# A three-stage attention and feed-forward kernel: a new order for TensorE, a new planner table, ones as letters of the order

## The chip, the cores and the metric

The kernel runs on one core of one Trainium2 chip. The metric is the device time of one execution in microseconds (us). Five engines work side by side, each through its own queue and in that queue's order: PE (TensorE, matmuls), DVE (VectorE), ACT (ScalarE), POOL (GpSimd) and SP (SyncE, which here only starts transfers).

## The reference

```python
q_pool = q.reshape(B, H, S // 2, 2, D).mean(axis=3)      # B=2, H=8, S=1152, D=64
scores = np.matmul(q_pool, k.transpose(0, 1, 3, 2)) / np.sqrt(D)
attn = np.exp(scores - scores.max(-1, keepdims=True))
attn = attn / (attn.sum(-1, keepdims=True) + 1e-09)
x = np.matmul(attn, v)                                   # 16 heads of 576 x 64
x = x.transpose(0, 2, 1, 3).reshape(1152, 512)
h = x @ moe_w_in                                         # 512 -> 2048
g = (a0 + a1*h + a2*h**2 + a3*h**3) / (1 + abs(b0)*abs(h) + abs(b1)*h**2 + 1e-06)
x = g @ moe_w_out                                        # 2048 -> 512
xn = x / sqrt(mean(x**2) + 1e-06) * rms_g
g = xn @ w_gate; val = xn @ w_val                        # 512 -> 1536 each
out = (g * sigmoid(g) * val) @ moe2_w_out                # 1536 -> 512
```

## The kernel before, in words

The program has an attention stage (to about 259 us in the profile), a first feed-forward stage, a normalisation and a second feed-forward stage. The feed-forward matmuls multiply pairs of numbers split into a high and a low half, three products each (`three`, L599).

Attention works on 16 heads in 8 pairs. A pair has 9 tiles of 128 query rows against 1152 keys, so there are 72 tiles, and two tiles are in flight at a time, each with its own three PSUM banks (`hid`, here `s_ps`). One tile goes: PE multiplies queries by keys (letters A and C of the order, L919); DVE takes the negated row maximum (`nm`, L951, 1152 columns); ACT takes the exponential with the row sum (`p`, L957); PE transposes the result in 64-column blocks (letters T and 2, L973); DVE and ACT copy the transposed blocks to `pt` (L1009 and L1006). When a head's 576 rows stand in `pt`, PE multiplies them by the values: nine steps a head, letter V (L1078, into the PSUM tile `av`). Before a head begins, its keys and its pooled queries are transposed on PE: letter P (L832; half of it goes to the bank `prep`, half to a corner of the second score tile's third bank), and each half is copied to `kT` or `qT` by DVE or ACT (`copy_ways`, L697 and L700). The pooled queries `qp` are one addition per head (L759). At a pair's end a row of reciprocals is transposed (L1111, L1125) to divide the output.

In the gaps DVE, ACT and POOL convert the weights of the later stages (`weight_ops`, `spill_ops`; tiles `wc`, `wraw`, `win_*`, `wout_*`, `spill`); none of this starts before the operation `later`, which is the exponential of tile 4.

The order of the work is planned when the program is built. Each piece of work is an `Op` with an engine (or several `ways`), an estimated cost, a due time and its dependences. `SHIFTS` moves the due time of each Op, `WAYS` fixes the way of some, and `order` emits the Ops one by one. PE's order in attention is not left to the planner: the string `PE_ORDER` gives it, one letter per Op, and each Op depends on the one before it. Where the string has `PTT2` (two tiles' transposes with no V ahead of them, at five places after the first tile), `attention` puts matmuls of a tile of ones by itself with no use for the result (`f_ones`, L1219): three ahead of the first T and two ahead of the second.

Two tiles are called a round below: round n holds tiles 2n and 2n+1, counted from 0.

Of the kernel before, what the change touches and what calls it, by code (L numbers as in the profile page):

```python
# [8 lines left out]
F32 = mybir.dt.float32  # L9
# [10 lines left out]
def attention_moe_moe2_kernel(  # L20
# [18 lines left out]
    nc = tc.nc  # L39
# [235 lines left out]
    def weight(w, u):  # L275
# [13 lines left out]
        "6QPGR_NgNPP@DORIESuPF?W6YP/LhPP]bRPOPkYN@Sc6ENPUPOePD8XJSTAU]dXyPidQdTwRbTt_PI>;SWlR8bSRPpPX[u(mSH(R"  # L289
        "d9X4PPUs3MyEPPRPPIyPONtQE]PyMKNPY]yFPPAX]UHPs^PKIZOVItBPHSQfJPn?Y*MZPKeK:PChPkBTKTLGXWPPPNV;]SGWbGPY"  # L290
        "TGIVOMSPPPPSPA?FM]FNP]CXPPhPPvPJLHST@PJPdPCsPp8PUZPHAWKVLL=KKSRUSJ?NRGPT_PPKwPUMERVHyyPMPVG]HD6PvDTP"
        "PYJE4UNg;KcN;GP<VD)P?PAKQSELPP]PRPYPZZPWQLUPKhPPYNAZPN>QOI(IQMPAYPPRBYDS@H[OVPGLPSQNSRS@SbfPQFLTMNGI"
        "QHa6PX[KNPPUUDMFS_PUWCPOUCPVPPPPbdJPJNPPPR:bW]FP@POrXMZ7PPXU[P4PDUXP_PRP@TbPWaPJQIOMGAVKHPAZPHM5VTJp"
        "?RTNRP3OVcPTN[gFLhJS[P6E(i`IPPIMPPCP@KL@S]_W1P_YNRoQPPPcFKDSjEH6HMdLXP>JEWUYU]OPP=cKKPnU]RL65@xXGWLR"
        "HPP1PPdK_On_RPWlITPQPKP[bMiPQWUQPb`N^WK;ZSQPQ<eOCMO>MIQPP]PVPPL_UR?:RIPXPKcV]PGPIPHSSPPPD[hPmPRPTPN;"
        "PRGPWQPUPkgUHBPcHGZJaZPXZRMZQQSPTNWPXHWJP(DP>?PQ)P=`NMY(PObNUTIbPNyRPNPQd]WK<PLPRPTE3GPYKOXSK?PPNPP;"
        "ZT@BCPSPi_TNNWPFb^ISJMISPPDPO[PLQPP8UYPPcPMnPITPPJLJKPTPPONPWPPRS:RPPDSPHJNPRSPNX4Z^PcP7DLOSPIHPPdPK"
        "MJeI`IPdPLKUPTWbTPEPRQlH]CZXHsaPPPPhK[PMUYQJhPGR)UePVT_RSKNS[PAeMEWPPPZQOPPcPXLSMaQ.QB]WTV_PPPSP?PKp"
        "^NPOCPPjNPIEFJWSSOGMQSPE`?PGPIPGUNQQM^HP](oYPPPjXXTP,J`APBMHEONHPWZONMQ>@ZX6PbPRPy[IOPNPPPPQmPSPQL^L"
        "XMOZLSLKFDYPIPmPPIHcrhZTXPD2MPWVP:UVPiYSCVO[SPUPSKP]PTITd<H[cOUODLGJPHPkCN6<XPCLPPLMPVPP6P]ZPPURGVTP"  # L300
        "KZY@bVPWPHPRVyZuPPPVK[APDkIPPUPPPIyYTuRDPVVI;MZjS_XM7[SHH?VyFL^IEP`VPSOR7PNPPPPPPE]MC7@ZVRZHQZPcPVB?"
        "Z>PWUIvPSR_JPPWcNaFV@]PO^HIYePPO@NPfRLTPQrWUPPUPmPY^GRKNPWcPTPYPJX;TP>PORPERQP<P]NZPPPPPPPPPPPNPyEKP"
        "PMPDDMYW_TP@[HPM[I<SMVKb`PP^PEZRAPPrLOXNP_@*?PQRPX^KYSBHPNPPQPJ=JTPQPPXPuJWvWPIGSPHPPIEODLID1PUWT^LQ"
        "PRPWPgPHNGLKFlP<KSC9FVCPLSDWP-KPPS]jQNyY6LE@PONTAU;JYP`UVQcPQKITPPPQAxPQdDP8y*AP6QOSFNPPPRTNDGJUeMHP"
        "PQ`DXKDFIKOKVI5BRR<hVB_PPYNNTPLhPPOK@GEPONTN^QSECEQPH1PRP@VPKP;ZXKPPHFTHSPPPYgKM(RXlPBNP[PLbmK:>NePX"
        "JQbPOPB:P`SUoPZ59UUVPUPX<KFkPYYQDZ[PGDyPyRBH<hf`M;LuK?LZLVPkUBTPQON>GOG3hPPYLPPOPRPP[[XhaPjZPCSTHPfN"
        "TX+Id8XPdPPPPGWTLbP0EPP8^MGEMOIPPPPO7(D7BDYPU_@YPJPUP^`PRHJPTPUUPOS]VPGPPPM8eLP<YPRNPP`SPPMFJQ;JKPKN"
        "MPPNPP`]KPPXXPPNPNOCQTPP(yVZJPPVBQP?JO(Q:aXPNPPPPIPaPFOM=XPUKRQCLL<QG:MDXXPPZPNobmfEO[P?WVQOPRPP]YPN"
        "DSP`PQGPPQE[SAP=PPMNvtPJT@PJQ=y`ddjPS?EFP_PVWPPOPPcLPJTMUJMGS^ZIG>mP.KWQSfQHMKRWQZPHUETWZRfSPJ>PPPPu"
        "NPFSNKPKnP7USRPQP:P_EV;[lDISSRLPPePFTTMPSPP1^=R[R]WXWJUjEMPJCVVPNZWAPKPVPTPcpJTBOdbGPPD]HRXPRPpQP[MS"  # L310
        "IPEQ6PPZKNKdGSOPrXSPPPXaPP[PPPGP[[HPa8PudKWU`PSPPQ_LSVPPP`DLPg]PPF=jPU_ULacKdPMPP^:jP)hJUXPWX=P^FTWH"
        "PMPUXLXLXUPFNUdPPPPsPPFNINPPQPP9LQ8RPHMPdPPPLJWDLTUHL]OMQQPSMPLSPDMPfVUXPPXYQPDyT]PPQPdRyZbPAWPPKBT;"
        "PC=PTTXL9PNPcQASWPYUHJEmYQdgOPP@BSN]PPMXP^/UP[PJPP9PeP^WNiPUUXYNMUPSE;(YPOL@HEL6SO_RCPOPiPS<nPNQMPW_"
        ";[PTPLMIP1OCyb-CP]PSC^P@i_PKFJMaGKON_OLPPQ?TkWO7NPPPPTqPPoLCFR]SNParDPJOPEWP,PNIP]NLQ@E7ePV]IOV;kNP]"
        "TPTPLPJPZ`MJTPPPHZAPKPPTTC"
# [1381 lines left out]
```

## Time and profile before

| | |
|---|---|
| median of 3 runs | 693.15 us (692.87 to 693.76) |
| the profiled execution | 692.14 us |
| its span, first to last instruction | 690.3 us |
| PE busy | 672.7 us, 97% of the span, 5457 instructions |
| DVE busy | 536.0 us, 78% |
| ACT busy | 406.7 us, 59% |
| POOL busy | 229.2 us, 33% |
| PE's granted clock, mean of the core | 0.998 of full speed |

Times are microseconds from the first instruction. A matmul's end is modelled in this profile, and matmuls overlap, so a stretch in which PE is "busy" need not be one in which it does as much as it could. An entry like `[1.61 <-ACT p L957]` says that the engine stood idle for 1.61 us before this instruction, and that the last thing it waited for was ACT's instruction of line 957 that writes `p`.

### The profile page before, as it was taken

What the parts mean: (1) busy time and instruction counts of PE and PEld (TensorE: products, weight loads), DVE (VectorE), ACT (ScalarE), POOL (GpSimd) and SP (SyncE); (2) the same over time, 40 slices, a digit from 0 to 9 for tenths busy, and PEclk for the clock granted to TensorE, in tenths of its full rate; (3) what the DMA queues carried; (4) which work ended last, traced back from release to release, by engine and by line L of the source; (5) the groups of instructions that cost most, each with busy time, mean ns of one, the idle gap of its engine ahead of it and who ended that gap; (6) DMA issues with size and microseconds to landing.
All of it is one profiled execution on the core that took longest, in us unless ns stands there. A gap on an engine that the chain in (4) does not pass through costs nothing.

```text
span 690.3 us, 13519 instructions
## 1 busy us (share of the span) xinstructions
PE 672.7 (97%) x5457; PEld 595.2 (86%) x5457; DVE 536.0 (78%) x706; ACT 406.7 (59%) x665; POOL 229.2 (33%) x226
## 2 busy tenths in 40 slices
PE   7899999999999999999999999999999999999998
PEld 6677777767767678999999999999999999989996
DVE  4789899898987978999897889667677257845744
ACT  3787888898889778997555666155233233311210
POOL 2125316756664652421111353055142011312200
PEclk9999999999999999999999999999999999999999
DMA  7433536676653525224115003201335012421103
GB/s 214 145 117 120 146 98 210 198 223 205 192 193 141 196 111 196 78 77 151 41 33 172 31 24 129 62 1 33 115 99 153 30 32 91 129 85 59 34 0 138
DMA packets 54062, 77.69 MB, mean 113 GB/s; under 512 B 6512, under 2 KB 36464, under 8 KB 54000
## 3 DMA queue, kind: packets, MB, share of 16 engines
q1 hardware_dynamic: 53712, 76.50, 34.3%
q8 instruction: 43, 0.70, 0.4%
q10 hardware_dynamic: 288, 0.33, 0.1%
q14 instruction: 19, 0.16, 0.1%
HBM read 62.40 MB, written 14.42 MB: 111 GB/s over the span
## 4 chain that ended last, share of the span: by engine, by line
PE 88%; DVE 6%; ACT 4%; issue 1%; DMA 1%; POOL 0%; SPq 0%; DVEq 0%; ACTq 0%; POOLq 0%
PE hid L599 35%; PE accp L599 25%; PE hid L919 10%; PE av L1078 9%; PE hid L973 7%; DVE nm L951 3%; ACT p L957 2%; DVE pt L1009 1%; PE hid L832 1%; PE prep L1125 1%; DMA qn<-in_q_dram 1%; PE prep L832 1%; DVE acc L1486 0%; DVE qp L759 0%; ACT m_p L1289 0%
## 5 line engine op out<-in xcount | busy, mean ns | idle before, releaser
L599 PE MATMUL hid<-x_hi,win_hi 128*128 128x384 f32 x480 | 161.6, 337 | 1.7 <-issue 0.9
L599 PE MATMUL hid<-x_hi,win_lo 128*128 128x384 f32 x480 | 160.6, 335 | 0.0
L599 PE MATMUL hid<-x_lo,win_hi 128*128 128x384 f32 x480 | 154.8, 335 | 0.0
L951 DVE TENSOR_REDUCE nm<-hid 128x1 f32<-128x1152 f32 x72 | 96.6, 1356 | 13.4 <-PE hid L919 10.2
L957 ACT ACTIVATE p<-hid,nm 128x1152 f32<-128x1152 f32 x72 | 87.9, 1221 | 29.3 <-DVE nm L951 26.6
L599 PEld LDWEIGHTS hid<-x_hi,win_hi 128*128 128x128 f32 x480 | 90.1, 188 | 3.6 <-issue 1.2
L919 PE MATMUL hid<-kT,qT 64*128 64x256 f32 (+3 forms) x800 | 91.3, 372 | 1.2 <-ACT qT L697 1.1
L599 PEld LDWEIGHTS hid<-x_lo,win_hi 128*128 128x128 f32 x480 | 89.6, 188 | 0.9
L599 PEld LDWEIGHTS hid<-x_hi,win_lo 128*128 128x128 f32 x480 | 90.1, 188 | 0.0
L973 PEld LDWEIGHTS hid<-ident,p 64*128 64x128 f32 x1296 | 52.6, 140 | 36.0 <-ACT p L957 21.9
L919 PEld LDWEIGHTS hid<-kT,qT 64*128 64x128 f32 (+1 forms) x800 | 73.7, 179 | 10.0 <-ACT qT L697 1.6
L1078 PE MATMUL av<-pt,vn 128*64 128x288 f32 x576 | 80.7, 415 | 0.0
L973 PE MATMUL hid<-ident,p 64*128 64x64 f32 x1296 | 66.0, 230 | 7.9 <-ACT p L957 6.4
L1337 POOL TENSOR_TENSOR g_lo<-m_p,g_hi 128x1152 fp32r<-128x1152 f32 (+1 forms) x16 | 37.4, 2342 | 108.1 <-ACT g_hi L1334 72.1
L1006 ACT ACTIVATE pt<-hid 128x512 f32<-128x512 f32 (+2 forms) x148 | 60.7, 441 | 8.7 <-PE hid L973 7.3
L599 PE MATMUL accp<-g_hi,wout_hi 128*128 128x384 f32 x192 | 64.4, 336 | 0.1
L599 PE MATMUL accp<-g_lo,wout_hi 128*128 128x384 f32 x192 | 64.3, 335 | 0.0
L599 PE MATMUL accp<-g_hi,wout_lo 128*128 128x384 f32 x192 | 64.2, 334 | 0.0
L174 ACT ACTIVATE wc<-wraw 128x512 f32<-128x512 f32 x68 | 45.7, 675 | 26.5 <-POOL win_lo L207 11.0
L1009 DVE COPY pt<-hid 128x512 f32<-128x512 f32 (+2 forms) x76 | 47.6, 633 | 16.1 <-PE hid L973 12.8
L1078 PEld LDWEIGHTS av<-pt,vn 128*64 128x64 f32 x576 | 37.0, 136 | 22.6 <-issue 0.7
L207 POOL TENSOR_TENSOR win_lo<-wc,win_hi 128x512 fp32r<-128x512 f32 x20 | 28.0, 1401 | 62.2 <-DVE win_hi L202 43.7
(133 smaller groups left out, 1229.4 us busy)
## 6 DMA issues: line engine op xcount, KB each, us to landing
wraw<-in_moe_w_out_dram SPq DMA_DIRECT2D x28, 512.0 KB, 3.6
far<-spill SPq DMA_DIRECT2D x23, 512.0 KB, 3.2
wraw<-in_moe_w_in_dram SPq DMA_DIRECT2D x16, 512.0 KB, 3.8
wraw<-in_moe_w_gate_dram SPq DMA_DIRECT2D x12, 512.0 KB, 3.6
wraw<-in_moe_w_val_dram SPq DMA_DIRECT2D x12, 512.0 KB, 3.6
vn<-in_v_dram SPq DMA_DIRECT2D x16, 288.0 KB, 3.0
kn<-in_k_dram SPq DMA_DIRECT2D x15, 288.0 KB, 4.1
qn<-in_q_dram SPq DMA_DIRECT2D x15, 256.0 KB, 3.4
```

The lines of the kernel that those rows point to most:

```text
L174: nc.scalar.activation(c.bitcast(F32), wt["raw", n][:, :, 1].bitcast(F32), AF.Abs, scale=2.0**-112)
L207: eng.tensor_sub(lo, w_float(n), hi.bitcast(F32))
L599: ins = nc.tensor.matmul(dst, lhsT=a[x], rhs=b[y], start=first and i == 0 and p == 0, stop=last and i == n - 1 and p == len(by) - 1,)
L832: ins = nc.tensor.transpose(e["prep", n_][r][:, at // 2:at // 2 + 64], src[rows], ident[rows, rows])
L919: ins = nc.tensor.matmul(ps[to, j, c:c + x1 - x0], lhsT=qT[2 * pr + h][rows, c0:c0 + to.stop - to.start], rhs=kT[2 * pr + h][rows, x0:x1], ...
L951: nc.vector.tensor_reduce(out=e["nm"], in_=scores(), op=ALU.max, axis=AX.X, negate=True)
L957: nc.scalar.activation(e["p"], scores(), AF.Exp, bias=e["nm"], scale=1.0, accum_out=sums[pr][:, t:t + 1])
L973: ins = nc.tensor.transpose(ps[:, g, c:c + 64], e["p"][rows, 128 * j:128 * j + 128], ident[rows, rows])
L1006: return nc.scalar.activation(to, src, AF.Copy)
L1009: return nc.vector.tensor_copy(to, src)
L1078: nc.tensor.matmul(e["av", h][64 * c:64 * c + 64, 0:QW], lhsT=v_tile[2 * pr + h][:, KEYS[kt], :], rhs=pt[pr, h][:, kt, c * QW:(c + 1) * QW ...
L1337: eng.tensor_sub(g_(1), p_(), g_(0).bitcast(F32))
```

## The change

Six things change. (1) `PE_ORDER` is another string. The nine V steps of a head stood in two rounds; now one head of four has them in three. Ahead of the transposes of rounds 0, 1, 2, 11, 20 and 29 no V stood; now that holds for rounds 0, 1 and 2 alone. (2) `SHIFTS` and `WAYS` are other tables, for all three stages. (3) The ones are a letter of the string, F: six Ops of three or two matmuls, in the first three rounds only; the rule that found `PTT2` is gone. (4) The matmuls of a P depend on both copies of the P before it (`split_copy`). (5) The first head's queries are loaded by two Ops in place of one. (6) `later` is the exponential of tile 1, and three estimated costs that the planner uses are other numbers (`w_shift`, `more=-35`, `more=75`).

```diff
-            ("ACT", 640, w_abs), ("ACT", 580, w_pm), ("DVE", Port(430), w_shift), ("DVE", Port(620), w_rest_kept),
+            ("ACT", 640, w_abs), ("ACT", 580, w_pm), ("DVE", Port(480), w_shift), ("DVE", Port(620), w_rest_kept),
...
     SHIFTS = (
-        "6QPGR_NgNPP@DORIESuPF?W6YP/LhPP]bRPOPkYN@Sc6ENPUPOePD8XJSTAU]dXyPidQdTwRbTt_PI>;SWlR8bSRPpPX[u(mSH(R"
+        "8L-TJ[PPUNOQVP>PKLU:WXUE?fPALDPn(JMPJP,9P>aSth<PPDQ8PfU(`QPSP=SU<OWjOMJLQVLDGPSKOPrQ=WPHSFaSkPW]MP<J"
...
     WAYS = (
-        ".....1.1...1......0.10.1.......0.11.....00..1.....10.1......00......0.0...0........1.........10...0."
+        "..........0.00.....1..0.1......00.0....0.0..00...0..1.........0.1......1...1.....11.1.......1..1...."
...
         if i == 0:
+            def load_q0():
+                src = q[b, h, 0:256].rearrange("(p r) d -> p r d", r=2)
+                nc.sync.dma_start(out=qn[s][:, 0], in_=src)
+            lq0 = Op("SP", 800, first - 34000, load_q0, [], [bq])
+            lq = Op("SP", 1750, first - 33900, lambda: load_q(1), [], [bq])
...
-                mm = Op(PE, 0.49 * at, kp, f_halves, [*deps, kq_mm.get(0)], [*bufs, *third[j], bk, bqp, *to])
+                mm = Op(PE, 0.49 * at, kp, f_halves, [*deps, kq_mm.get(0), *split_copy], [*bufs, *third[j], bk, bqp, *to])
...
-                    copy_ways(to_half, from_half, at // 2, True, 0.5 * float(D) ** -0.5 if what == "q" else None, seen=seen_half),
+                    copy_ways(to_half, from_half, at // 2, True, 0.5 * float(D) ** -0.5 if what == "q" else None, seen=seen_half, more=-35),
...
-                added.append(op_any(copy_ways(to_, src_, QW, True), key + 100 * c, [last], [ab, xb]))
+                added.append(op_any(copy_ways(to_, src_, QW, True, more=75), key + 100 * c, [last], [ab, xb]))
...
     PE_ORDER = (
-        "CACAPTT2AC2ACPTT2AC2ACPTT2A2CACPVVVTVV2TAC2ACPVVVTVT2A2CACPVVVVVTT2AC2ACVVVVTT2AC2ACPVVVVVTT2A2CACPV"
+        "ACCAFFTPT2AC2ACPFFTT2AC2ACPFTFT2A2CACPVVVVTVT2AC2ACPVVVTVT2AC2ACPVVVTVVT2AC2ACVVVVTT2AC2ACPVVVVTVT2A"
...
+        for x in range(6):
+            n = (3, 2)[x % 2]
+            o = Op(PE, 213 * n, x // 2 * 2 * TS, lambda n=n: f_ones(n), [kq_mm[-1]], [Buf("av")])
+            o.mode = "rows"
+            queue["F"].append(o)
...
-        idle, t = [], 0
-        for x in range(len(seq)):
-            t += PE_ORDER[x] == "T"
-            if t > 1 and PE_ORDER[x:x + 4] == "PTT2":
-                idle += [(seq[x], seq[x + 1], 3), (seq[x + 1], seq[x + 2], 2)]
...
-    later = sum_op[0][4]
+    later = sum_op[0][1]
```

How the instructions move, at three places. The first is DVE's queue at the start, from the first head's pooled queries to the first two row maxima (`nm`); `qn_152` holds the second head's raw queries. Before:

```order
L759 TENSOR_TENSOR qp<-qn_148 128x128
L759 TENSOR_TENSOR qp<-qn_148 128x512
L700 TENSOR_SCALAR kT_200<-hid 128x256
L700 TENSOR_SCALAR kT_200<-hid 128x128
L951 TENSOR_REDUCE nm<-hid 128x1 x2
```

Now:

```order
L767 TENSOR_TENSOR qp<-qn_148 128x128
L767 TENSOR_TENSOR qp<-qn_148 128x512
L767 TENSOR_TENSOR qp<-qn_152 128x640
L963 TENSOR_REDUCE nm<-hid 128x1 x2
```

The two copies of keys have gone to ACT, and the addition for the second head, which POOL did, stands ahead of the first row maximum. In SP's queue the second head's two key loads now stand ahead of its two query loads.

The second is PE's queue ahead of and in the transposes of tiles 22 and 23 (round 11), from the key preparation's last blocks on. Before (`av<-ones` is the matmul of ones):

```order
L832 MATMUL prep<-ident,kn 128x64
L832 MATMUL hid<-ident,kn 128x64
L1219 MATMUL av<-ones 128x128 x3
L973 MATMUL hid<-ident,p 128x64 x17
L1219 MATMUL av<-ones 128x128 x2
L973 MATMUL hid<-ident,p 128x64 x18
```

Now (six matmuls of `av<-pt,vn` are three V steps; `ident,rx` are the transposes of reciprocals):

```order
L840 MATMUL prep<-ident,kn 128x64
L840 MATMUL hid<-ident,kn 128x64
L1090 MATMUL av<-pt,vn 64x288 x6
L1123 MATMUL av<-ident,rx 128x128
L985 MATMUL hid<-ident,p 128x64 x17
L1137 MATMUL prep<-ident,rx 128x128 x4
L985 MATMUL hid<-ident,p 128x64 x18
```

Three V steps have come from other rounds to this place and the five matmuls of ones have left it; the same holds for rounds 20 and 29.

The third is PE's queue in the normalisation: `ones,m_u` sums the squares of a third of the tokens, `ident,small` spreads that third's factors, and `hid<-x_hi` are the first matmuls of the second feed-forward stage. Before:

```order
L1454 MATMUL hid<-ones,m_u 128x1 x3
...
L599 MATMUL accp<-g_hi,wout_hi 128x384
...
L1480 MATMUL hid<-ident,small 128x128 x3
...
L1454 MATMUL hid<-ones,m_u 128x1 x3
L599 MATMUL hid<-x_hi,win_hi 128x384
```

Now:

```order
L1460 MATMUL hid<-ones,m_u 128x1 x3
...
L1460 MATMUL hid<-ones,m_u 128x1 x3
...
L1486 MATMUL hid<-ident,small 128x128 x3
...
L1486 MATMUL hid<-ident,small 128x128 x3
L599 MATMUL hid<-x_hi,win_hi 128x384
```

Between the first sum and the first spread stood 12 output matmuls (`accp`), and 21 more behind the spread; now 9 and a second sum stand between them, and 6 behind.

## Rows read from the trace of the kernel before

**Rows 1.** Busy time in steady attention; columns PE, PEld (weight loads), DVE, ACT, POOL, clock, DMA share.

```profile
28.00:248.00 220.00, 214.21 (x2759) 158.79 (x2756) 194.59 (x275) 186.58 (x378) 109.89 (x119) 1.00 0.51 166
```

**Rows 2.** The exponential's line: count, least/median/greatest ns, first and last start.

```profile
L957 ACT ACTIVATE p<-hid,nm x72: 1205/1221/1226, 10.0 to 247.7; 128x1152 f32<-128x1152 f32 x72
```

**Rows 3.** Timeline of ACT: first exponentials of rounds 10, 12, 19, 21, 28 and 30.

```profile
77.71 1.22 ACT L957 ACTIVATE p<-hid,nm 128x1152 f32<-128x1152 f32 x1 [1.16 <-DVE nm L951]
91.47 1.22 ACT L957 ACTIVATE p<-hid,nm 128x1152 f32<-128x1152 f32 x1 [0.56 <-DVE nm L951]
138.08 1.22 ACT L957 ACTIVATE p<-hid,nm 128x1152 f32<-128x1152 f32 x1 [0.47 <-DVE nm L951]
151.56 1.22 ACT L957 ACTIVATE p<-hid,nm 128x1152 f32<-128x1152 f32 x1
199.16 1.22 ACT L957 ACTIVATE p<-hid,nm 128x1152 f32<-128x1152 f32 x1 [0.97 <-DVE nm L951]
213.30 1.22 ACT L957 ACTIVATE p<-hid,nm 128x1152 f32<-128x1152 f32 x1 [0.26 <-DVE nm L951]
```

**Rows 4.** Groups of instructions, 28 to 248 us: count | busy, mean ns | idle before them.

```profile
L951 DVE TENSOR_REDUCE nm<-hid 128x1 f32<-128x1152 f32 x66 | 88.6, 1356 | 9.2 <-PE hid L919 6.3 <-PE hid L832 1.7
L1009 DVE COPY pt<-hid 128x512 f32<-128x512 f32 (+2 forms) x69 | 42.8, 627 | 13.3 <-PE hid L973 10.1 <-ACT p L957 1.5
```

**Rows 5.** Timeline of ACT: first exponentials of rounds 0, 1 and 2.

```profile
10.00 1.22 ACT L957 ACTIVATE p<-hid,nm 128x1152 f32<-128x1152 f32 x1 [2.33 <-DVE nm L951]
17.45 1.22 ACT L957 ACTIVATE p<-hid,nm 128x1152 f32<-128x1152 f32 x1 [1.06 <-DVE nm L951]
23.88 1.22 ACT L957 ACTIVATE p<-hid,nm 128x1152 f32<-128x1152 f32 x1 [0.99 <-DVE nm L951]
```

**Rows 6.** Busy time by stretch at the start; columns as in rows 1.

```profile
9.00:12.40 3.40, 1.52 (x33) 1.15 (x29) 2.79 (x4) 2.40 (x4) 1.54 (x1) 1.00 1.01 299
12.40:15.80 3.40, 3.16 (x29) 2.82 (x31) 1.23 (x2) 1.76 (x6) 0.00 (x0) 0.50 0.59 144
```

**Rows 7.** Timeline of PE: transposes of tiles 0 and 1, three matmuls of ones (two records each).

```profile
11.36 0.77 PE L973 MATMUL hid<-ident,p 64*128 64x64 f32 x17 [1.61 <-ACT p L957]
12.64 0.58 PE L973 MATMUL hid<-ident,p 64*128 64x64 f32 x6 [0.50 <-ACT p L957]
17.14 0.88 PE L1219 MATMUL av<-ones 64*128 64x128 f32 x6
```

**Rows 8.** Timelines of SP, POOL and DVE at the start: key loads, second head's addition, first maximum.

```profile
3.42 0.59 SPq L733 DMA_DIRECT2D kn<-in_k_dram  x1
4.05 0.44 SPq L734 DMA_DIRECT2D kn<-in_k_dram  x1
6.76 1.54 POOL L759 TENSOR_TENSOR qp<-qn 128x640 f32<-128x640 f32 x1 [4.95 <-DMA qn<-in_q_dram]
8.61 1.36 DVE L951 TENSOR_REDUCE nm<-hid 128x1 f32<-128x1152 f32 x1 [1.75 <-PE hid L919]
```

**Rows 9.** DVE groups by form, 30 to 240 us: the addition and the copy that change engine.

```profile
L759 DVE TENSOR_TENSOR qp<-qn 128x640 f32<-128x640 f32 x2 | 2.7, 1340 | 0.0
L700 DVE TENSOR_SCALAR qT<-hid 128x320 f32<-128x320 f32 x6 | 2.9, 481 | 0.0
```

**Rows 10.** PE's waits in steady attention, 28 to 248 us: us in total, times, longest.

```profile
PE av L1219 <- ACT rxh L1115: 1.2, 1, 1.2
```

**Rows 11.** PE's waits from 248 us to the end.

```profile
PE hid L599 <- issue: 0.9, 1, 0.9
PE hid L599 <- DVE m_p L1295: 0.9, 1, 0.9
```

**Rows 12.** Timelines of the normalisation: first sum and first spread on PE, high halves on ACT.

```profile
452.10 0.80 PE L1454 MATMUL hid<-ones,m_u 128*128 128x1 f32 x6
454.94 0.49 PE L1480 MATMUL hid<-ident,small 128*128 128x128 f32 x3
456.12 1.05 ACT L1489 ACTIVATE x_hi<-acc 128x384 fp32r<-128x384 f32 x2 [0.32 <-DVE acc L1486]
```

More of the change, by code (lines that the diff above doesn't have):

```diff
@@ L294, in attention_moe_moe2_kernel @@
[L294 to L303, printed above, removed]
@@ L700, in on @@
             seen(eng.tensor_scalar(dst(), src(), by, 1.0, op0=ALU.mult, op1=ALU.mult))
-        ways = [(ACT, cost(ACT, n), on_act), (DVE, 80 + 1.06 * n if psum else Port(80 + 0.52 * n), lambda: on(nc.vector))]
+        ways = [(ACT, cost(ACT, n) + more, on_act), (DVE, 80 + 1.06 * n + more if psum else Port(80 + 0.52 * n), lambda: on(nc.vector))]
         if not psum:
@@ L734, in load_k, with load_q @@
             queue.dma_start(out=e["k"][:, NKT], in_=src[:, NKT - 1])
-        def load_q():
+        def load_q(u0=0):
             full = NFULL * 256
             src = q[b, h, 0:full].rearrange("(u p r) d -> p u r d", p=128, r=2)
-            for u0, u1 in ((0, 1), (1, NFULL)) if i == 0 else ((0, NFULL),):
-                nc.sync.dma_start(out=qn[s][:, u0:u1], in_=src[:, u0:u1])
+            nc.sync.dma_start(out=qn[s][:, u0:NFULL], in_=src[:, u0:NFULL])
             nc.sync.dma_start(out=qn[s][tail[s], NFULL], in_=q[b, h, full:].rearrange("(p r) d -> p r d", r=2))
@@ L763, in head_ops @@
             m1 = 2 * D
-            o_q0 = Op(DVE, Port(cost(DVE, m1)), key, lambda: f_add(nc.vector, 0, 1), [lq], [bq, bqp])
+            o_q0 = Op(DVE, Port(cost(DVE, m1)), key, lambda: f_add(nc.vector, 0, 1), [lq0], [bq, bqp])
             o_qa = op_any(
@@ L852, in head_ops @@
             kq_mm[0] = mm
+            if i == 0 and n_ == 2:
+                kq_mm[-1] = mm
             outs = []
@@ L1176, in attention, with f_ones @@
                 pair_ops(i // NT)
-        queue = {c: [] for c in "ACT2VP"}
+        def f_ones(n):
+            ps = T("av", [128, 512], F32, space=PSUM)
+            for _ in range(n):
+                nc.tensor.matmul(ps[:, 0:128], lhsT=ones[0:64], rhs=ones[0:64], start=True, stop=True)
+        queue = {c: [] for c in "ACT2VPF"}
+        for x in range(6):
[3 more added lines that the diff above has]
+            queue["F"].append(o)
         for i in range(NP * NT):
@@ L1214, in attention_moe_moe2_kernel @@
         early_h[u] = project_ops("in", u, (NP * NT + 6 * u) * TS, free)
-    def f_ones(n):
-        ps = T("av", [128, 512], F32, space=PSUM)
-        for _ in range(n):
-            nc.tensor.matmul(ps[:, 0:128], lhsT=ones[0:64], rhs=ones[0:64], start=True, stop=True)
-    for x, y, n in idle:
-        o = Op(PE, 213 * n, x.key, lambda n=n: f_ones(n), [x], [Buf("av")])
-        o.mode = "rows"
-        y.deps.append(o)
     order(80)
```

105 lines of the change are left out of this document (59 added, 46 removed).

## The prediction

> **What bounds the kernel now.** I read the busy shares first, then attention's exponentials one by one, then the waits of the engines there, then the start, then PE's waits behind attention. From 278 us on PE waits for almost nothing: from 248 us to the end the list of its waits has two places of 0.9 us, and little besides [rows 11]. The change neither adds nor removes a matmul there, so only attention, the start and these two places can give time.
>
> In steady attention four engines are nearly full at once: of 220 us PE is busy 214.2, DVE 194.6, ACT 186.6 [rows 1]. PE's 97% overstates it, since matmuls overlap and their ends are modelled: its weight loads fill 158.8 us of the same stretch, 72%. The better measure is the length of a round, from one first exponential to the next. Between the first and last of the 72 exponentials lie 237.7 us for 35.5 rounds, 6.70 us each [rows 2]. Rounds 10 and 11 together took 13.76 us, rounds 19 and 20 13.48, rounds 28 and 29 14.14 [rows 3]: 6.90 us a round. These are the stretches in which one set of transposes has no V steps ahead of it. A round with no V work on PE is thus not shorter; what makes a round is the ring of score, row maximum, exponential, transposes and copy, and its busiest link is DVE. Yet DVE also stands idle 22.5 us before its row maxima and copies, and 18.1 us of that ends on PE (10.1, 6.3 and 1.7) [rows 4]. So PE and DVE hold each other up, and neither is a plain bound.
>
> The Trainium skill says the like ("Perfetto Trace Analysis", Identifying the Most-Contended Engine): matmul busy time is a poor measure of headroom, and weight-load time is better. By a PE bound the V-free rounds would be worth the 5.7 us of the second rival; by the page, and by the length of the rounds, far less.
>
> **The change, term by term.** A minus is a gain.
>
> *Clock at the start, -1.0.* Round 0 lasts 7.45 us from first exponential to first exponential, round 1 6.43 [rows 5]. In between PE's clock was granted at half, 1.2 instead of 2.4 GHz, from 12.4 to 15.8 us [rows 6], after PE had stood idle for 1.61 us and again for 0.50 us around the transposes of tile 0 [rows 7]. Two F letters now stand in the first of these gaps: five matmuls of ones, of which three take 0.88 us [rows 7], so some 1.5 us; and the second head's key preparation moves to the second gap. If the clock stays up, round 0 becomes like round 1: 1.0 less. Ends: 0, and 1.6, half of the 3.16 us of PE work done at half clock [rows 6].
>
> *First row maximum, +0.5.* It started at 8.61 us [rows 8]. DVE now adds the second head's queries ahead of it, 1.34 us by the row of the same addition on DVE [rows 9]. Their load landed just before 6.76 us, when POOL could start [rows 8]; two key loads of 0.59 and 0.44 us of issue [rows 8] now stand ahead of it on SP's queue, so it lands near 7.8 and the addition ends near 9.1: 0.5 late. Ends: -0.3 (the keys copied by ACT let PE begin its first scores that much sooner, and the load comes no later) and +1.0 (the key loads also slow the query load).
>
> *The three V-free places, -1.2.* Six rounds at 6.90 against 6.70 [rows 2, 3] are 0.2 x 6 = 1.2. One part can be named: a matmul of ones needs the tile `av`, and once it waited 1.2 us in PE's queue for ACT to read that tile, with the transposes behind it [rows 10]. Ends: 0, and 5.7 if PE were the bound (three times about 1.5 us of ones, plus the wait of 1.2 us [rows 7, 10]).
>
> *V steps spread, -1.0.* Before the last round 135 V steps stood in 30 rounds, 4.5 each; now in 33, 4.1 each. If the 18.1 us that DVE waits for PE shrink with them, by 9%, that is 1.6; I take 1.0, as a shorter wait is not always passed on. Ends: 0 and 1.6.
>
> *Two additions back to POOL, -0.4.* Two of the pooled-query additions in steady attention were DVE's, 1.34 us each [rows 9]; POOL, busy half of that time [rows 1], has them now. Ends: 0 (DVE waited for something else anyway) and 2.7; I stay near the lower, as there are only two.
>
> *More copies on DVE, +1.0.* Counted over DVE's order, attention now holds eight more key or query copies from the score bank and two fewer from `prep` (6), two more `xt`, three fewer `x_hi`, four more weight halves: 9 net, priced at 0.48 us [rows 9], and two more `pt` copies at 0.63 [rows 4]: 5.6 us. DVE has 25.4 us free in 220 [rows 1], and with `later` moved up part of the weight work falls into rounds 1 and 2, where it had room. Ends: 0 and 5.6; I take a fifth.
>
> *Entry to the feed-forward stage, -0.8.* PE waits 0.9 and 0.9 us for DVE to leave the score banks of the first two blocks [rows 11]. DVE's queue in the last round is one weight step, two `xt` copies and an `x_hi` shorter, so it starts on those blocks earlier. Ends: 0 and 1.8; half of it taken.
>
> *Normalisation, +0.3.* From first sum to first spread lie 2.84 us, and from the spread to the end of the first high half 1.7 (452.10, 454.94, 456.12 plus half of 1.05) [rows 12]. The covers ahead of the spread suffice; behind it six output matmuls and a spread, some 1.3 us, now stand where 21 stood. PE waits about 0.4 there. Ends: 0 and 0.8.
>
> *At nothing:* the wait of a P for both copies of the P before (they end a round earlier, and P writes the banks that they read in any case); earlier weight loads (the DMA engines are busy half of the time [rows 1]); the new order in the feed-forward stages, as PE's work is the same.
>
> Sum: -1.0 + 0.5 - 1.2 - 1.0 - 0.4 + 1.0 - 0.8 + 0.3 = -2.6. The profiled execution took 692.14 us and would take 689.5; the median of the runs is 1.0 above it, so the median becomes **690.5 us**.
>
> **Rivals.** *The clock falls anyway: 691.5.* Between the ones and the transposes of tile 0 a gap of over a microsecond stays. For it speaks that it fell in this place before, behind two gaps of this kind. The Trainium skill ("TensorE: Matmul & The Clock Gate", Part 1) says that the monitor behind the clock runs free of the kernel's start, so that the count of slow matmuls differs from run to run; no row here shows a second run.
>
> *PE is the bound: 686.0.* Then the V-free term is 5.7 in place of 1.2. Against it stand rounds without V that are no shorter.
>
> *The ring sets every round, and nothing moves: 692.6.* Then only the start counts, -1.0 + 0.5. For it: rounds of 6.70 whatever stands in them.
>
> *DVE becomes the bound: 695.5.* Its place is the steady part: 5.6 us of new copies less 2.7 us of additions are 2.9; the V terms, the entry and POOL's help give nothing; with the start, +2.4. It decides once the copies fall in rounds whose DVE has no gap: 220 - 194.6 us over 33 rounds are 0.77 us each, and a round that gets two more copies (0.96) has spent them. Against it: 18.1 of these gaps are waits for PE, which shrink.
>
> **How the numbers follow.** Forecast 0.40 (own range 688.0 to 691.7), clock falls 0.10, PE bound 0.06, nothing moves 0.23, DVE bound 0.21. A measurement of this kernel tells 0.2%, 1.4 us, from no change: below 691.8 is faster, above 694.5 slower. The first three cases are faster: 0.56; same 0.23; slower 0.21. The range, 687.0 to 695.4, leaves out the PE bound, the far end of the gains and the upper half of the DVE case, under 0.2 in all.
>
> **What would show it.** Right: clock 1.00 from 12.4 to 15.8 us; first maximum near 9.1; rounds 10, 11, 19, 20, 28, 29 near 6.7 and the mean round near 6.6; no wait of ones for `rxh`; under 1 us of waits at 268 to 278. Wrong: DVE above 92% of steady attention with rounds of 6.8 or more; waits of the transposes for `p` that grow; over 1 us of PE idle between 450 and 470.

## The result and the profile after

The changed kernel took **697.86 us** (median of 6 runs, 695.92 to 699.90) where the kernel before took 693.25 (6 runs, 691.91 to 693.76): a ratio of 1.0074, interval 1.0055 to 1.0092. It is slower by 4.6 us. The forecast was 690.5, a gain, with a range to 695.4: the time moved the other way and lies outside the range.

| | before | after |
|---|---|---|
| profiled execution, its span | 692.14, 690.3 us | 699.27, 697.5 us |
| to the end of round 3's first exponential | 31.67 us | 36.58 us |
| from there to the end of round 35's | 215.95 us | 215.78 us |
| from there to the last instruction | 442.7 us | 445.1 us |
| PE's granted clock, mean | 0.998 | 0.992 |

The span grew by 7.2 us, more than the medians did, since the profiled run of before was among the short ones and that of after among the long ones. Of the 7.2, 4.9 lie in the first three rounds, none in steady attention, and 2.4 behind it.

**The first rounds.** The timeline of ACT of the changed kernel, first exponentials of rounds 0 to 3 (start, duration, what ended the idle time before):

```profile
10.03 1.22 ACT L969 ACTIVATE p<-hid,nm 128x1152 f32<-128x1152 f32 x1 [2.81 <-DVE nm L963]
20.10 1.20 ACT L969 ACTIVATE p<-hid,nm 128x1152 f32<-128x1152 f32 x1
28.25 1.22 ACT L969 ACTIVATE p<-hid,nm 128x1152 f32<-128x1152 f32 x1 [0.90 <-DVE nm L963]
35.36 1.22 ACT L969 ACTIVATE p<-hid,nm 128x1152 f32<-128x1152 f32 x1 [1.23 <-DVE nm L963]
```

Round 0 begins where it did [rows 5], but round 1 begins at 20.10 where it began at 17.45, and its exponential waits for nothing: something else held ACT. The timeline of all engines, 13 to 22 us, with the rows that matter:

```profile
13.46 0.38 SPq L739 DMA_DIRECT2D qn<-in_q_dram  x1
13.88 1.38 SPq L740 DMA_DIRECT2D qn<-in_q_dram  x1
...
15.30 0.59 SPq L95 DMA_DIRECT2D coef<-in_moe_a_dram  x1
15.93 0.43 SPq L96 DMA_DIRECT2D coef<-in_moe_b_dram  x1
...
18.05 0.17 DVE L100 TENSOR_SCALAR ncoef<-coef 128x4 f32<-128x4 f32 x1 [1.78 <-DMA coef<-in_moe_a_dram]
18.16 1.36 DVE L963 TENSOR_REDUCE nm<-hid 128x1 f32<-128x1152 f32 x1
...
19.99 0.20 ACT L103 ACTIVATE absb<-coef 128x2 f32<-128x2 f32 x1 [4.75 <-DMA coef<-in_moe_b_dram]
...
21.45 1.22 PE L985 MATMUL hid<-ident,p 64*128 64x64 f32 x17 [3.62 <-ACT p L969]
```

With `later` the change moved the loads of the feed-forward stage's constants into round 1, and with them their two users: `ncoef` on DVE between the row maxima of round 1, `absb` on ACT ahead of round 1's first exponential. Nothing in attention needs either. The loads were issued behind a query load that waited for POOL, and `absb` held ACT for 4.75 us; the exponential behind it kept PE waiting 3.62 us. The clock fell in that wait. Busy time by stretch, columns as in [rows 6]:

```profile
12.40:15.80 3.40, 3.14 (x46) 2.83 (x48) 2.64 (x4) 2.07 (x7) 1.03 (x1) 1.00 0.30 89
20.98:27.81 6.83, 6.10 (x62) 4.56 (x64) 3.07 (x5) 4.38 (x10) 0.00 (x0) 0.50 0.71 229
276.98:280.40 3.42, 3.42 (x12) 3.42 (x11) 3.42 (x9) 3.31 (x7) 0.26 (x1) 0.50 0.00 0
```

In this execution the stretch from 12.4 to 15.8, at half before, has the full 2.4 GHz, as forecast. But in the wait of 3.62 us the clock falls, and 6.8 us run at 1.2 GHz; behind a wait at the entry to the feed-forward stage another 3.4 do. These rows are of one long execution: in another of the same start (run 5) the price is far smaller.

**Steady attention** is the same to 0.2 us. From round 3 to round 35, before and then after, busy time in the columns of [rows 1]:

```profile
31.67:247.62 215.95, 210.25 (x2715) 155.95 (x2711) 191.31 (x271) 183.92 (x371) 108.78 (x119) 1.00 0.51 166
```

```profile
36.58:252.36 215.78, 210.53 (x2679) 151.67 (x2677) 192.51 (x280) 176.22 (x354) 113.73 (x125) 1.00 0.52 167
```

**Behind attention.** PE's waits from 248 us on, after; before they were 0.9 and 0.9 [rows 11] and about 0.2 in the normalisation:

```profile
PE hid L599 <- DVE m_p L1301: 1.8, 1, 1.8
PE hid L599 <- DVE x_lo L1502: 0.2, 1, 0.2
PE hid L1486 <- POOL small L1482: 0.2, 1, 0.2
PE hid L599 <- DVE acc L1492: 0.2, 1, 0.2
```

The wait at the entry is one of 1.8 in place of two that add up to the same; the new cost there is the clock behind it, in this execution. The profiles of runs 1 and 3 have the same wait of 1.8 and no fall behind it; they take 443.9 us from round 35 to the end, where this one takes 445.1. The normalisation waits 0.4 more. And in the last round the second exponential starts 2.06 us after the first (251.14, 253.20), where it was 1.26 (246.40, 247.66).

### The profile page after: what moved, and what is told of

Same layout as the page of the kernel before. It is cut to its first block, busy times and chain, and to the rows that moved or that the text cites. A ratio compares the mean times of both kernels' runs of the same rounds, so it can differ in the third digit from the quotient of the medians.

```text
span 697.5 us, 13454 instructions
## 1 busy us (share of the span) xinstructions
PE 677.7 (97%) x5437; PEld 594.4 (85%) x5437; DVE 545.0 (78%) x720; ACT 398.9 (57%) x648; POOL 225.6 (32%) x229
## 4 chain that ended last, share of the span: by engine, by line
PE 82%; DVE 8%; ACT 6%; DMA 2%; issue 1%; SPq 1%; POOL 0%; DVEq 0%; ACTq 0%; POOLq 0%
PE hid L599 34%; PE accp L599 25%; PE hid L931 8%; PE av L1090 7%; PE hid L985 6%; ACT p L969 4%; DVE nm L963 4%; DMA qn<-in_q_dram 1%; DVE pt L1021 1%; PE hid L840 1%; DMA coef<-in_moe_b_dram 1%; DVE acc L1492 0%; PE prep L840 0%; ACT pt L1018 0%; PE prep L1137 0%
## 5 line engine op out<-in xcount | busy, mean ns | idle before, releaser
L931 PE MATMUL hid<-kT,qT 64*128 64x256 f32 (+3 forms) x800 | 94.3, 377 | 1.2 <-DVE pt L1021 0.6
L1090 PE MATMUL av<-pt,vn 128*64 128x288 f32 x576 | 83.1, 417 | 0.0
L1343 POOL TENSOR_TENSOR g_lo<-m_p,g_hi 128x1152 fp32r<-128x1152 f32 (+1 forms) x13 | 28.2, 2173 | 112.7 <-ACT g_hi L1340 97.5
L1021 DVE COPY pt<-hid 128x512 f32<-128x512 f32 (+2 forms) x78 | 49.2, 635 | 14.6 <-PE hid L985 11.8
L207 POOL TENSOR_TENSOR win_lo<-wc,win_hi 128x512 fp32r<-128x512 f32 x22 | 29.9, 1360 | 66.5 <-ACT win_hi L200 43.1
```

The costliest lines, as they stand in the source:

```text
L207: eng.tensor_sub(lo, w_float(n), hi.bitcast(F32))
L931: ins = nc.tensor.matmul(ps[to, j, c:c + x1 - x0], lhsT=qT[2 * pr + h][rows, c0:c0 + to.stop - to.start], rhs=kT[2 * pr + h][rows, x0:x1], ...
L1021: return nc.vector.tensor_copy(to, src)
L1090: nc.tensor.matmul(e["av", h][64 * c:64 * c + 64, 0:QW], lhsT=v_tile[2 * pr + h][:, KEYS[kt], :], rhs=pt[pr, h][:, kt, c * QW:(c + 1) * QW ...
L1343: eng.tensor_sub(g_(1), p_(), g_(0).bitcast(F32))
```

## The experiments

All but two (4 and 8) start from the changed kernel. In most, the planner's order stays word for word and only the place of single steps in the emitted order is changed, by a table "step: the step behind which it is issued":

```diff
+    PUT_OFF = {1071: 206, 1072: 206}
...
-            op.fn()
+            if op.at in PUT_OFF:
+                waiting.append(op)
+            else:
+                op.fn()
+            for o in [o for o in waiting if PUT_OFF[o.at] == op.at]:
+                waiting.remove(o)
+                o.fn()
```

Step 1071 is `negate_coef`, 1072 `abs_b`, 206 the exponential of tile 4. Unless said otherwise a run has 10 executions; beside runs 1, 2 and 4 to 9 the kernel before gave 693.04 (31 executions, runs 1 and 4 to 6) and 693.01 (31, runs 2 and 7 to 9).

**1. The constants' users moved back** (the table above).

> The changed kernel with one edit: the two instructions that use the loaded constants (the negation on DVE, the absolute value on ACT) are issued behind round 2's work, where the kernel before has them; their loads and every other instruction stay where the change put them. Theory A (these two wait for the loads at the head of DVE's and ACT's queues, and round 1's second row maximum and its first exponential stand behind them): first exponential of round 1 near 17 us in place of 20.1, no 3.6 us wait of PE for it, rounds 0 to 2 together 20.5 to 22 us in place of 25.3, clock 1.0 from 20.9 to 27.8, time 692.5 to 694.5. Rival B (the earlier loads themselves, and the weight work behind them, fill the queues): the same wait under other names, 697 to 698. Rival C (only the wait goes, the clock falls all the same): 694.5 to 696.

Measured: 693.85 us, ratio to before 1.0015 (0.9996 to 1.0033). Theory A: two instructions of 0.2 us account for 4.0 of the 4.6 us. The first exponentials of rounds 0 to 3:

```profile
10.55 1.22 ACT L978 ACTIVATE p<-hid,nm 128x1152 f32<-128x1152 f32 x1 [3.26 <-DVE nm L972]
16.82 1.22 ACT L978 ACTIVATE p<-hid,nm 128x1152 f32<-128x1152 f32 x1 [1.06 <-DVE nm L972]
24.59 1.22 ACT L978 ACTIVATE p<-hid,nm 128x1152 f32<-128x1152 f32 x1 [0.55 <-DVE nm L972]
32.54 1.22 ACT L978 ACTIVATE p<-hid,nm 128x1152 f32<-128x1152 f32 x1 [1.65 <-DVE nm L972]
```

The wait is gone; the three rounds take 22.0 us in place of 25.3 (20.5 in the kernel before). In this execution the clock fell for 3.4 us at 28.2, so it was not quite spared.

**2. The loads earlier, the users where the change has them.**

```diff
+            if op.at == 48:
+                load_consts()
-            op.fn()
+            if op.fn is not load_consts:
+                op.fn()
```

> The changed kernel with one edit: on SP's queue the three loads of constants stand ahead of the query load that waits for POOL's addition (the one issued at 13.46 us in the changed kernel's profile, the constants at 15.30); their two users stay ahead of round 1's row maximum and exponential, where the change put them. Theory A (what costs is how late the loads land behind that wait, not the place of their users): the loads are issued near 10.5 to 11 us, land by 15, the users wait for nothing, rounds 0 to 2 take 20.5 to 22 us, and the time is that of the run with the users moved back, 693 to 694.8. Rival B (any user of a load at the head of these queues costs, wherever the load stands): 696.5 to 698.

Measured: 693.44 us, ratio 1.0010 (0.9994 to 1.0025): theory A. Step 48 is the query load that waits for POOL. SP and ACT:

```profile
10.63 0.43 SPq L95 DMA_DIRECT2D coef<-in_moe_a_dram  x1
11.10 0.43 SPq L96 DMA_DIRECT2D coef<-in_moe_b_dram  x1
...
15.39 0.20 ACT L103 ACTIVATE absb<-coef 128x2 f32<-128x2 f32 x1
```

`absb` stands in the same place and waits for nothing; rounds 0 to 2 take 19.5 us (exponentials at 10.29 and 29.82). So the price is neither the instruction nor its place alone, but a load that lands late with a queue behind it.

**3. Both cures.** The table of 1 and the early loads of 2 (12 executions).

> The changed kernel with both cures of the start: the constants' loads ahead of the query load that waits for POOL, and their two users behind round 2's work. Theory A (one wait, cured by either edit): no more than 0.3 us better than the loads alone (693.44), 693.0 to 693.6, still level with the kernel before. Rival B (each edit takes away a part of its own): 691.5 to 692.7, under the kernel before.

Measured: 693.42 us, ratio 1.0007 (0.9996 to 1.0018), beside 693.29 of before. Theory A: one wait, and either edit cures it. No version with the whole work in it beat the kernel before.

**4. The same move in the kernel before.** Its loads issued behind tile 0's copies, its two users ahead of round 1's maximum and exponential.

```diff
+            if op.at == 173:
+                op.fn()
+                load_consts()
+            elif op.at == 187:
+                abs_b()
+                op.fn()
+            elif op.at == 195:
+                negate_coef()
+                op.fn()
+            elif op.at not in (1063, 1064, 1065):
+                op.fn()
```

> The kernel before with one thing moved: the three constant loads are issued ahead of the key loads of the head after next, right behind tile 0's copies, and their two users ahead of round 1's second row maximum (DVE) and of round 1's first exponential (ACT), as in the changed kernel. Theory A: the first exponential of round 1 moves from 17.5 to near 20 us or later, time 3 to 5.5 us over the kernel before, 696 to 698.7. Rival B (the loss belongs to the new order of PE's work and the later query load): within 1 us of the kernel before.

Measured: 693.83 us, ratio 1.0014 (0.9992 to 1.0035): theory A's number was wrong, and rival B's (within 1 us) is the one that came. Of rival B's reason the rows support the later load:

```profile
12.86 0.59 SPq L95 DMA_DIRECT2D coef<-in_moe_a_dram  x1
13.50 0.43 SPq L96 DMA_DIRECT2D coef<-in_moe_b_dram  x1
...
17.21 0.20 ACT L103 ACTIVATE absb<-coef 128x2 f32<-128x2 f32 x1 [0.87 <-DMA coef<-in_moe_b_dram]
```

Here SP reaches the loads at 12.86 us, not 15.30, and `absb` waits 0.87 us, ahead of an exponential that is due then anyway. In the changed kernel POOL's addition of the third head's queries starts at 11.89 (10.84 before), the query load that waits for it is issued at 13.46 (12.41 before), and one of its two issues took 1.38 us. The move is the same in both kernels; the later start of the loads in the changed one made it dear, and that varies by execution, as run 5 shows.

**5. DVE's order at the entry.** `PUT_OFF = {1675: 1695, 1674: 1695}`: two steps of the first block behind the one that frees its last bank.

> The changed kernel with one edit: on DVE, at the entry to the feed-forward stage, the two steps of the first block that no bank waits for (L1329 at 270.97 us, L1323 at 274.22 us) are issued behind the last step that frees the first block's score banks (L1301 at 274.69 us). Theory A (DVE's order holds the banks): PE's wait of 1.79 us at 273.65 falls to 0.6 to 1.0, the clock stays at 1.0 from 277.0 to 280.4, and from round 35's exponential to the end it takes 2 to 2.7 us less than 445.1; time 695 to 696.3. Rival B (ACT's steps set the pace there, DVE would only stand idle): the wait stays over 1.5 us, time 697.5 to 698. Rival C (wait shorter, clock falls all the same): 697.0.

Measured: 696.86 us, ratio 1.0050 (1.0028 to 1.0072), 1.0 under the changed kernel, but the two intervals overlap, and the reason given is not borne out. PE's waits from 248 us on:

```profile
PE hid L608 <- DVE m_p L1310: 1.3, 1, 1.3
PE hid L608 <- issue: 0.9, 1, 0.9
```

The wait shrank and a second one came behind it, as in the kernel before. From the first feed-forward matmul to the end it takes 441.5 us, in run 1, with the wait of 1.8 and the clock up there, 441.0. What theory A promised from the order alone did not come.

This profile (of the shortest of the ten executions, 694.41 us) also shows the changed kernel's start a second time, as the edit touches nothing there (timelines of SP and ACT, then the clock in the columns of [rows 6]):

```profile
14.45 0.43 SPq L96 DMA_DIRECT2D coef<-in_moe_b_dram  x1
...
18.09 0.20 ACT L103 ACTIVATE absb<-coef 128x2 f32<-128x2 f32 x1 [1.25 <-DMA coef<-in_moe_b_dram]
```

```profile
12.40:15.81 3.41, 2.99 (x41) 2.81 (x38) 1.87 (x3) 2.16 (x6) 0.41 (x1) 0.50 0.44 138
```

Here the second constant load is issued at 14.45 us, not 15.93, `absb` waits 1.25 us, not 4.75, and round 3's first exponential ends at 32.46 us, not 36.58. So what the two users cost depends on when the load lands in that execution. And the clock is at half from 12.4 us on, with the ones in place.

**6. Edits 1 and 5 together.**

> Both edits together, the constants' two users behind round 2 and DVE's order at the entry. If the two places hold all of the loss and are independent, the gains add: 5 and 2.4 us off 697.9, 690 to 691.5, which would be 2 us or more under the kernel before. If the steady rounds give time back when the start is earlier (a ring that runs against a later due transfer), 692.5 to 694.

Measured: 695.23 us, ratio 1.0030 (1.0012 to 1.0048): worse than edit 1 alone by 1.4. The gains do not add; beside edit 1, edit 5 is a loss. The profiles show 0.6 of it, from round 35 to the end (444.5 us against 443.9).

**7. Without the first five matmuls of ones.** Run 1 with the first two F Ops empty.

```diff
-            for _ in range(n):
+            for _ in range(n if x > 1 else 0):
```

> The run with the users moved back (693.85 us), less the first two sets of ones, five matmuls ahead of the transposes of tile 0. Theory A (these ones keep the clock at 1.0 behind tile 0): most runs have a clock below 1.0 and the median is 1.0 to 1.7 us above 693.85. Rival B (the clock falls once in the first 32 us whatever stands there, here or two rounds later): the spread of clocks as before, median within 0.6 us of 693.85.

Measured: 695.89 us, ratio 1.0036 (1.0019 to 1.0052), 2.0 above run 1, on theory A's side and more than its 1.0 to 1.7. In the profile the clock falls behind tile 0 again:

```profile
13.17:16.58 3.41, 2.92 (x37) 2.79 (x35) 1.88 (x3) 2.15 (x6) 0.00 (x0) 0.50 0.41 96
```

Not all of the 2.0 is the clock's. In every other run an execution takes 1.7 to 1.9 us more than its span; here it takes 1.74 to 2.78, and the median span, 693.2 us against run 1's 692.05, is only 1.15 longer. Round 0 shows the price of the fall: 7.5 us with it, 6.3 in run 1 without. But the fall behind tile 0 also comes with the ones in place, at 12.09 us in the profile of run 3, 12.40 in run 5 and 12.61 in run 9, so that they do not hold the clock there for certain.

**8. Ones in the kernel before.** `ONES = {170: 5, 179: 2}`: so many matmuls of ones ahead of the transposes of tiles 0 and 1.

> The kernel before with one thing added: five matmuls of ones in PE's gap ahead of the transposes of tile 0, two in the gap ahead of those of tile 1; nothing moved. Theory A (the ones keep the clock): clock 1.0 from 12.4 to 15.8, more runs at a clock of 1.0, median 691 to 692.2 against 693.04. Rival B (the clock falls in one of the next rounds instead): 692.7 to 693.3. Rival C (the ones are in front of the transposes and delay them): up to 693.8.

Measured: 693.07 us, ratio 1.0005 (0.9993 to 1.0017): rival B by its number. The start did get shorter (round 3's first exponential ends at 30.26 us, not 31.67), but the profile has the clock fall elsewhere:

```profile
12.40:15.80 3.40, 3.35 (x50) 2.98 (x51) 2.42 (x3) 1.86 (x6) 0.18 (x1) 1.00 0.39 101
86.54:89.95 3.41, 3.41 (x33) 3.13 (x31) 1.96 (x6) 2.22 (x7) 0.00 (x0) 0.50 0.31 84
147.98:151.39 3.41, 3.41 (x27) 3.06 (x25) 2.04 (x4) 2.48 (x8) 1.42 (x2) 0.50 0.30 104
```

**9. The last round's V steps.** Run 1 with `1038: 1023, 1042: 1027` added to the table.

> The run with the users moved back (693.85 us) with one more edit: in the last round the V step that the change put ahead of the last tile's scores stands behind them, and the one ahead of the last tile's transposes behind those. Theory A (these two V steps hold up the last exponential): from round 35's first exponential to its second 1.3 us as in the kernel before in place of 2.06, to the first matmul of the feed-forward stage 2.4 to 2.5 in place of 2.9, median 693.2 to 693.5. Rival B (POOL and the copies of the last pair end last there anyway): 2.9 stays, 693.6 to 694.1.

Measured: 694.39 us, ratio 1.0021 (1.0007 to 1.0036), 0.5 above run 1, with overlapping intervals. The two exponentials come 1.85 us apart (2.06 in run 1, 1.26 in the kernel before), but the first feed-forward matmul starts 3.6 us behind the end of the first of them, where run 1 has 2.9: the V steps taken from ahead of the last tile's scores and transposes fill PE behind them (four matmuls at 251.57 us, the first feed-forward one at 252.20). The rows (timeline of ACT):

```profile
247.41 1.22 ACT L978 ACTIVATE p<-hid,nm 128x1152 f32<-128x1152 f32 x1 [0.49 <-DVE nm L972]
249.26 1.22 ACT L978 ACTIVATE p<-hid,nm 128x1152 f32<-128x1152 f32 x1 [0.55 <-DVE nm L972]
```

Neither theory fits; what the last round costs stays open.

**10 to 14. What sets steady attention.** All on run 1, one execution each, read from round 3's exponential to round 35's. In all ten profiles of kernels with all of attention's work in them and no fall of the clock there, this stretch took 215.7 to 216.0 us.

*Half of the V matmuls.* `for c in range(2 if kt in (0, NKT - 1) else 1):`

> The run with the users moved back, leaving out one of the two matmuls in seven of every nine V steps (the output of attention's second key half is then incomplete): about 200 of some 520 V matmuls between rounds 3 and 35, 0.145 us each by the changed kernel's rows (75.2 us for 518), 29 us of PE work less; nothing else is touched. Read from round 3's exponential to round 35's, 215.8 us in every version so far. Theory A (the ring of scores, maximum, exponential, transposes and copies sets the round; V fills PE's time beside it): 211 to 216. Rival B (PE is the bound, so that V steps have a price wherever they stand): 187 to 195.

Measured: 215.76 us. That decides nothing, as the rows of V show, with the same steps first in run 1 and then here:

```profile
109.70 1.19 PE L1099 MATMUL av<-pt,vn 128*64 128x288 f32 x8
```

```profile
109.63 1.18 PE L1099 MATMUL av<-pt,vn 128*64 128x288 f32 x4
```

Eight matmuls and four take as long. The two of a V step write the two halves of `av`'s 128 partitions, and together they cost what one does.

*A lighter DVE.* `w_shift` leaves out the weights that go to memory, `w_rest_kept` is empty.

> The run with the users moved back, leaving out two of DVE's steps for the weights that go back to memory (the shift and the OR of the low word; those weights are then wrong): about 20 x 0.44 and 20 x 0.69, 22 us of DVE work less between rounds 3 and 35; nothing else is touched. Theory A (the ring sets the round, and DVE's row maxima and copies are links of it that other DVE work delays only now and then): 208 to 214 in place of 215.8. Rival B (DVE is the bound of steady attention): 194 to 199. Rival C (DVE has room, its other work costs nothing): 215 to 216.

Measured: 215.96 us with 20.6 us less DVE time: rival C. DVE's own waits show where it went (34 to 249 us; run 1 had 6.8 and 3.1 in these two places):

```profile
33.97:249.93 215.96, 210.08 (x2679) 151.42 (x2677) 172.04 (x237) 175.66 (x354) 114.42 (x125) 1.00 0.52 168
```

```profile
DVE pt L1028 <- PE hid L992: 18.1, 37, 1.2
DVE nm L970 <- PE hid L938: 7.0, 14, 1.2
```

*A shorter row maximum.* `in_=scores()[:, 288:1152]`

> The run with the users moved back, with every row maximum taken over 864 of the 1,152 columns (the first 288 are left out, so the subtracted maximum can be too small); each maximum takes about 1.05 us in place of 1.355, 64 of them between rounds 3 and 35. Theory A (the row maximum is a link of the ring, and both tiles of a round have theirs in series with the rest): two times 0.3 us a round, 32 rounds, 10 to 19 us less than 215.8, 197 to 206. Rival B (the maxima of the two tiles overlap with the other tile's links, and only one of them counts): 206 to 212. Rival C (another engine's order of work, not the ring, sets the round): 215 to 216, as with half of the V matmuls.

*Three of nine V steps left out whole.* `for c in range(0 if kt in (2, 4, 6) else 2):`

> The run with the users moved back, leaving out three of every nine V steps whole, both matmuls (a third of the keys is then missing from the output). With half of the matmuls the rows of V kept their length (1.19 us for eight as for four), so that run took no time from PE; this one does: about 86 V steps of 0.27 us between rounds 3 and 35, 23 us of PE. Theory A (the ring sets the round): 212 to 215.8 from round 3 to round 35. Rival B (PE is the bound in most rounds, as its rows without gaps say: 210.6 of 215.8 us are covered): 193 to 204. Between them, 204 to 212, both share the rounds.

*Both.*

> The same with the shorter row maximum as well (864 of 1,152 columns, 1.05 us in place of 1.355). Theory A (ring): as the short maximum alone, 212.4, or less by no more than what the skipped steps alone gave. Rival B (PE is the bound, the ring is right behind it): the maximum, worth 3.4 us alone, is worth more once PE has room, 6 to 15 us under the run with the skipped steps alone. Rival C (two independent bounds): the gains of the two just add, 3.4 us under it.

Measured: 212.36 us with the shorter maximum, 213.80 with a third of V gone, 204.20 with both. In this order, busy time in the columns of [rows 1]:

```profile
31.37:243.73 212.36, 209.62 (x2679) 151.95 (x2677) 177.00 (x280) 176.76 (x355) 113.75 (x125) 1.00 0.54 170
```

```profile
31.79:245.59 213.80, 191.18 (x2501) 139.93 (x2497) 192.27 (x280) 175.30 (x355) 113.51 (x125) 1.00 0.52 168
```

```profile
31.00:235.20 204.20, 190.45 (x2503) 139.99 (x2499) 177.58 (x280) 175.00 (x355) 113.73 (x125) 1.00 0.55 176
```

Against run 1's 215.83, taking 19 us from PE gives 2.0, taking 0.3 us from each of 64 maxima, 19 in all, gives 3.5, and both give 11.6, twice the sum. The shorter maximum falls just short of its rival B (206 to 212), the V steps alone agree with their theory A, and the pair with its rival B: with PE relieved, the maximum is worth 9.6 in place of 3.5. The simplest reading is two limits within 2 to 4 us of each other: PE's own work, covered for 210.6 of 215.8 us, and the ring of scores, maximum, exponential, transposes and copies. The DVE work that the lighter run left out is in neither.

## Why the prediction was wrong

**The step that failed** is the one "at nothing": "earlier weight loads (the DMA engines are busy half of the time)". Moving `later` moves every step that depends on it, and I priced only the transfers. The constants' loads depend on it too, and their two users then stood at the head of DVE's and ACT's queues, ahead of links of the ring; I did not ask what was queued behind them. The trace of before held a warning: there too the two `coef` loads took 2.8 and 4.0 us from issue to landing, so that users at the head of a queue soon behind their loads had to wait. Runs 1 and 2 put it, in the medians, at 4.0 to 4.4 us, all but 0.2 to 0.6 of the loss; in single executions `absb` held ACT for 4.75 us or for 1.25 (run 5).

**Clock at the start (-1.0):** the size was right, the certainty was not. A fall in round 0 costs about 1.2 us there (7.5 us against 6.3, runs 7 and 1). In the profiled execution of the changed kernel it stayed away and the clock fell at 20.98 us, in the new wait; that the wait alone brings that fall is not shown, as in the run with the lighter DVE, without this wait, the clock fell at 20.47. In the profiles of runs 3, 5 and 9 it fell behind tile 0 in spite of the ones. The rival "the clock falls anyway" comes nearer: run 8 bought a shorter start and no time.

**First row maximum (+0.5):** 0.0 between these two profiles. The queries landed at 7.9 us, as reckoned (7.8), but the addition took 0.82 us where I took 1.34, the mean of two unlike additions in steady attention, so the maximum started at 8.64 us, 0.03 later [rows 8]. One pair of executions does not settle this term: with the same order of DVE it started at 8.6 to 9.6 us in the profiles of runs 1 to 3, 5 and 6, and with that of the kernel before at 8.4 (run 8) and 9.8 (run 4).

```profile
7.90 0.82 DVE L767 TENSOR_TENSOR qp<-qn 128x640 f32<-128x640 f32 x1 [2.03 <-DMA qn<-in_q_dram]
8.64 2.62 DVE L963 TENSOR_REDUCE nm<-hid 128x1 f32<-128x1152 f32 x2
```

**V-free places (-1.2), V steps spread (-1.0), additions to POOL (-0.4), copies on DVE (+1.0):** together -1.6, measured -0.2. The base was misread: the last half of the 35.5 rounds that I divided by was only the 1.26 us between round 35's two exponentials, so the mean round is 6.75 us (215.95 over 32), not 6.70, and the six rounds stood 0.9 above it, not 1.2. These six now take 40.9 us where they took 41.4, 0.5 less, and the other rounds gave 0.3 back. The wait of ones for `rxh` did go [rows 10], and rounds still vary, from 5.9 to 7.9 us (6.2 to 7.4 before). The reason given in the prediction, that PE and DVE hold each other up, had two errors. DVE's total of work is no bound: 20.6 us of weight steps left out gave nothing. What the added copies cost, and what the additions gave, no run tells by itself. And "the ring's busiest link is DVE" set PE aside: by the last three runs PE's covered time is close to a limit, a hair from the ring's, and moving V steps about takes work from neither. The rival "nothing moves" was right for this part.

**Entry to the feed-forward stage (-0.8):** 0 in waits (1.8 against 0.9 and 0.9), and in the profiled run a fall of the clock on top. The shorter queue of DVE in the last round did not shorten the wait; run 5 shows that the order there trades one wait for another. And the stretch grew where I priced a gain: without a fall of the clock, runs 1 and 3 take 443.9 us from round 35 to the end, the kernel before 442.7; 0.5 of that comes ahead of the first feed-forward matmul, 0.7 behind it.

**Normalisation (+0.3):** 0.4 in waits, right.

Of the rivals, "DVE becomes the bound" gave the nearest time, for a reason that the run with the lighter DVE refutes. None of them was the mechanism that decided.

What the runs leave open: why the last round of the changed kernel is 0.8 us longer between its exponentials, and the 0.1 to 0.8 us by which the cured versions still stand above the kernel before, which their intervals don't tell from nothing. At an equal clock the gap is plainer: at a mean clock of 1.000 nine executions of runs 1 to 3 have a median of 693.16 us (692.00 to 693.51), eight of the kernel before 690.84 (690.78 to 691.05). Of these 2.3 us the 1.2 behind round 35 are located, the rest is not; the cured versions hide it by more executions without a fall, 9 of 32 against 8 of 79. Neither `later` nor the table's share of the feed-forward stage was put back by itself.

## What to carry to other kernels

When a dependence is moved, list every step that hangs on it, also those of 0.2 us, and ask of each what it waits for and what stands behind it in its engine's queue; a load that lands late costs nothing until an instruction waits for it at the head of a busy queue. Keep users of a load away from the head of such a queue, or issue the load ahead of anything on its own queue that can wait. Before counting gains in a steady stretch, find out whether one limit sets it or two: where two stand close together, relieving either is worth next to nothing.

## What was not expected

- Where the clock falls differs from execution to execution of one kernel. In run 8 it fell at 86.5 and 148.0 us, each time for 3.41 us at 1.2 GHz and with PE busy throughout; right before each, PE had stood idle for 0.7 and 0.4 us ahead of transposes, in the V-free rounds 11 and 20 of that order:

```profile
83.10:86.54 3.44, 2.35 (x43) 1.97 (x41) 3.22 (x6) 2.89 (x5) 0.00 (x0) 1.00 0.38 105
```

  With these two falls its steady attention took 218.2 us in place of 215.95, 1.1 for each. The 62 executions of the kernel before beside runs 1, 2 and 4 to 9 have these medians by mean clock: 690.84 us at 1.000 (8 executions), 692.77 at 0.998 (28), 693.06 at 0.995 (17), 694.22 at 0.992 (7), 696.32 at 0.990 (2). At 0.992 the changed kernel took 696.96 to 699.27 (4 executions), 2.7 to 5.1 above 694.22, so at an equal clock it still loses. By this one execution the V-free places can have a price in the clock that the forecast did not name; the change takes three of them away. How often the clock falls there was not measured.
- Two V matmuls that write different halves of `av`'s 128 partitions take the time of one: 1.19 us for eight, 1.18 for four.
- The 1.34 us of [rows 9] is a mean of two unlike additions. One took 0.82 us with POOL idle, as did the one at the start of the changed kernel; the other took 1.86, with POOL at work on a weight step of its own. Runs 4 and 8 have the same two lengths. That POOL's step is the cause no run tests (timelines of DVE and POOL, kernel before):

```profile
92.96 0.82 DVE L759 TENSOR_TENSOR qp<-qn 128x640 f32<-128x640 f32 x1
166.74 1.86 DVE L759 TENSOR_TENSOR qp<-qn 128x640 f32<-128x640 f32 x1
166.64 1.28 POOL L235 TENSOR_TENSOR spill<-wc,spill 128x512 fp32r<-128x512 f32 x1
```

- One issue of a load on SP took 1.38 us where the same load's issue mostly takes 0.52.
